# Float64 weights joined and split in pairs, and a new order for the first two halves of the program

## The chip, the core and the metric

The kernel runs on one core of one Trainium2 chip. The metric is the time of one execution on the device, in microseconds (us); the figure quoted is the median of several runs. Five engines take part: TensorE (PE in the profile, with its weight loads as PEld), VectorE (DVE), ScalarE (ACT), GpSimd (POOL) and SyncE (SP), which only issues DMAs. Each engine works through its own queue in the order in which the program was written; where one needs another's result it waits on a semaphore, and everything behind it in its queue waits too.

## The reference

The computation is a linear attention with a decaying state, followed by a layer with three up-projections, a maximum over them and a down-projection:

```
B, H, S, D = 4, 8, 768, 48            # attention: r, k, v, w (B, H, S, D), u (H, D)
for t in range(S):
    cur = u * k[t] (outer) v[t]
    y[t] = r[t] @ (state + cur)
    state = w[t][:, None] * state + k[t] (outer) v[t]
x = y.transpose(0, 2, 1, 3).reshape(3072, 384)
h = max(max(x @ w1, x @ w2), x @ w3)  # w1, w2, w3: (384, 768)
out = h @ w_out                       # w_out: (768, 384)
```

The four weight matrices arrive as float64, the rest as float32.

## The kernel before

**The parts.** Time is cut into 6 chunks of 128 steps; with 4 batches that makes 24 attention units, k = 0 to 23. Four units make 512 rows of x, one of the six "halves" of the second layer. A half has 18 up groups (6 column blocks of 128 by the three matrices; a group is 3 or 9 matmuls with 512 columns) and 8 down steps. The program begins with fillers (`warmer`, L613: matmuls on a tile of zeros whose result nobody reads). The attention of units 0 to 11, all of the weights' preparation and the first two halves of the second layer are then written out in an order given by a table of step names, `PARTS`; a loop writes the other four halves afterwards.

**Attention steps** (one letter and the unit's number). On VectorE `b`, `p`, `q`, `f`, `r`: a scan backwards (L401), a floor, an inverse, a scan forwards (L416), a product (L425); `d` and `e`: the diagonal terms (L436, and on TensorE L451, two-column matmuls); `M` copies the scores into the tile `a` (L489 on VectorE, L493 on ScalarE). On TensorE `T`: transposes (L504), `X`: scores (L482), `U`: gain of the state (L538 or L529), `R`: the state's part of the result (L517), `V` and `Y`: the two parts of scores times values (L572), with a small copy on ScalarE (`touch`, L578) between them. `E` copies the result y into x on ScalarE (L590); after units 1, 3 and 7 it also sends six small DMAs x<-x (L598) that move rows within x, three from SP's queue and three from ScalarE's in the first half, all six from SP in the second. `n` and `e` load the inputs of later units. The attention units need nothing of the weights.

**Weights.** 24 chunks of 128x384, 18 for the up groups and 6 for the down steps. For each: `w` loads the raw 64-bit words into a room of 128 x 768 words (L304); `l` converts two 16- and 32-bit parts on ScalarE (L319, L320) into a tile `cv`; `c` (function `weights`) puts the sign into one part on VectorE for this chunk (`head_w`, L333), and joins the two parts of the chunk before into a float32 value (`join_w`, L344) in a further room that two neighbours share. The first four column blocks of the first half (12 up groups and 4 down chunks) multiply these float32 values with plain x ("plain" groups, steps `gd`, `gc` on 256 columns and `ge` on 512). All others need the value split in two: `s` writes the upper part on ScalarE (L132) and, one `s` later, the remainder on VectorE (L133). `FIX` is the order of the splits: the chunks that the first half needs split come first, those of the plain groups last. x itself is split by `x`.

**Rooms.** 25 rooms of 128 x 2 x 384 words are handed out from a list; `cv` has three buffers of two parts.

A plain group is written as

```
for n, (ct, (wt, part)) in enumerate((ct, term) for ct in range(KT) for term in terms):
    nc.tensor.matmul(ps[:, cols], lhsT=wt[i][:, ct * 128:(ct + 1) * 128], rhs=x[part][:, ct, cols], ...)
```

with one term if it is plain and three (L167, x_hi and x_lo) if it is split.

Of the kernel before, what the change touches and what calls it, by code (L numbers as in the profile page):

```python
# [29 lines left out]
F32 = mybir.dt.float32  # L30
# [3 lines left out]
U16 = mybir.dt.uint16  # L34
# [41 lines left out]
PARTS = """b0 w p0 W2 d0 q0 b1 w f0 p1 e0 r0 W11 R0 q1 d1 c0 T0 f1 X0 w e1 M0 W4 V0 r1 Y0 n3 d2 X1 b2 U0 p2 q2 l E0 e2 f2 c  # L76
           l M1 T1 R1 c r2 n4 c1 S0 b3 W10 V1 Y1 E1 d3 p3 R2 w X2 M2 q3 T2 f3 w U1 S1 w c2 r3 W6 w V2 e3 l Y2 c3 b4 c w W5
           X3 l E2 T3 d4 M3 n5 W3 l R3 U2 S2 l c V3 gd1 p4 w c gd0 q4 f4 t r4 gd3 Y3 l w c t w t E3 Z4 l c e4 b5 gd4 t p5
           d5 q5 T4 n6 l c c4 w gd2 gd5 l X4 U4 t f5 m4 c S4 w w M4 t U3 gc0 r5 t gc3 t c gc1 S3 l b6 c p6 R4 V4 q6 T5 t e5
           l c5 w w l Z5 X5 Y4 U5 l f6 m5 S5 c d6 c M5 Z6 gc7 gc8 c t l t n7 w E4 gd8 c ge10 t gd7 t t b7 p7 l r6 s w ge11  # L80
           w gc4 l c s e6 t d7 l T6 q7 t w c R5 f7 n8 c6 V5 X6 U6 gd6 Y5 m6 S6 w E5 r7 s t M6 e7 c x s l gc6 c T7 R6 V6 c t
           l gc2 s c X7 t U7 w Y6 E6 ge9 l t gc5 ge13 l b8 t w ge14 d8 p8 c w l s l q8 c M7 Z7 m7 S7 ge15 t ge12 t c f8 c7
           t ge16 t r8 c R7 s T8 V7 X8 U8 s n9 s t t Y7 e8 ge17 D0 E7 b9 D2 D1 p9 n10 c8 x s Z8 d9 m8 S8 s D3 M8 s q9 s D4
           D5 D6 D7 G12 b10 s f9 s G14 r9 c9 p10 G5 t T9 t s s q10 R8 n11 V8 e9 t X9 U9 f10 Y8 s G13 E8 Z10 Z9 G16 m9 S9 t
           b11 G3 d10 G15 r10 s t c10 G17 T10 t e10 p11 R9 M9 s V9 X10 U10 t Y9 t m10 S10 d11 G0 t G2 q11 t E9 f11 G1 n12
           G4 b12 r11 T11 p12 M10 X11 R10 V10 n13 t U11 q12 t t e11 d12 Z11 t f12 s G6 m11 t t S11 s r12 G8 s Y10 t M11 t
           c11 G11 t e12 s E10 G9 G10 t T12 t b13 p13 G7 q13 d13 t R11 V11 X12 s U12 Y11 t f13 n14 H0 E11 r13 c13 H2 M12 H1
           Z13 H3 Z12 H4 c12 m12 x S12 T13 H6 H5 H7 e13"""
# [5 lines left out]
FIX = [*range(3 * FR, 3 * FT), *range(3 * FT + FR, NW), *range(3 * FR), *range(3 * FT, 3 * FT + FR)]  # L94
# [14 lines left out]
def kernel(ctx: ExitStack, tc, tin, nat, u_flat, u_pair, v_t, w_flat, out, ytr):  # L109
# [16 lines left out]
    whi, wlo, wval = {}, {}, {}  # L126
    sums = const.tile([128, LINE], F32, name="sums")
# [87 lines left out]
    left, spot = {}, NW  # L215
# [6 lines left out]
    with ExitStack() as fast:  # L222
# [11 lines left out]
        cv_p = pool("cv", 3)  # L234
# [52 lines left out]
        stage = {}  # L287

        loaded, home, held = 0, {}, []
# [5 lines left out]

        def load_w():
# [5 lines left out]
            raw = raw[:, :, :].rearrange("p a b -> p (a b)")  # L302
            raw = raw.bitcast(U16) if wide else raw[:, 0:PC]
            nc.sync.dma_start(out=raw, in_=shifted(i) if wide else w_all[i])  # L304
            stage[i] = raw

        lows = {}
        begun = 0

        def low():  # L310

            nonlocal begun
            if wide and begun < NW:
                while loaded <= begun:
                    load_w()
                body = stage[begun].bitcast(U32).rearrange("p (n t) -> p n t", t=2)[:, :, 0]
                head = stage[begun].rearrange("p (n t) -> p n t", t=4)[:, :, 2]
                cv = cv_p.tile([128, 2, PC], U32, name="cv")
                nc.scalar.activation(out=cv[:, 0, :], in_=head, func=AF.Relu, scale=8.0, bias=low_end[:, :])  # L319
                nc.scalar.activation(out=cv[:, 1, :], in_=body, func=AF.Relu, scale=2.0 ** -13 * (1.0 - 1.05 * 2.0 ** -20))  # L320
                lows[begun] = cv
                begun += 1

        def head_w(i):

            if not wide:
                wval[i] = stage.pop(i)
                home.pop(i)
                return
            if i not in lows:  # L330
                low()
            head = stage.pop(i).bitcast(U32).rearrange("p (n t) -> p n t", t=2)[:, :, 1]
            nc.vector.scalar_tensor_tensor(out=lows[i][:, 0, :], in0=head, scalar=0x8000, in1=lows[i][:, 0, :],  # L333
                                           op0=ALU.bitwise_and, op1=ALU.bitwise_or)

        def join_w(i):

            if not wide:
                return
            if i % 2 == 0:  # L340
                pairs[i // 2], pair = room()
                wval.update((i + j, pair[:, j, :]) for j in range(2))
            cv = lows.pop(i)
# [28 lines left out]
        def split_w3(i):  # L372

            w = room(F32R)[1]
            whi[i], wlo[i] = w[:, 0, :], w[:, 1, :]
            split(whi[i], wlo[i], wval[i], wrest)
# [562 lines left out]
```

## Time and profile before

| | before |
|---|---|
| median of 3 runs | 404.03 us (403.25 to 404.46) |
| the profiled execution | 403.82 us |
| its span, first to last instruction | 401.9 us |
| TensorE busy in the span | 392.3 us, 98% |
| VectorE busy | 269.8 us, 67% |
| ScalarE busy | 169.7 us, 42% |
| GpSimd busy | 84.4 us, 21% |
| granted TensorE clock, mean | 0.996 |

The profile comes from one execution. "Busy" of TensorE counts the fillers as well as the work. The span is shown in 40 slices of about 10 us as tenths, and any stretch can be asked for by its own window; a timeline lists instructions in order of time, like ones merged in one row. What an engine waited for is inferred from semaphores; "issue" is a wait that no semaphore of the profile explains.

### The profile page before, as it was taken

The page shows a single profiled execution, that of the slowest core. Times are in us where ns is not written, and L with a number is a line of the kernel's source. Part 1 is how long each engine was busy: PE and PEld are TensorE (multiplying, and loading weights), DVE is VectorE, ACT ScalarE, POOL GpSimd, SP SyncE. Part 2 cuts the span into 40 slices and gives each one's busy share as a digit, 9 for nine tenths or more (in the row PEclk, how much of TensorE's full clock was granted, in tenths as well). Part 3 has the DMA queues.
Part 4 walks back from the last instruction along what each step waited for, and adds up shares of the span by engine and source line. Part 5 has one row for each costly group of instructions (what it writes and reads, how often), then busy time and mean ns, then how long its engine had stood idle before and what let it go on. Part 6 is the DMA issues. An engine that isn't in the chain of part 4 may idle for free.

```text
span 401.9 us, 10388 instructions
## 1 busy us (share of the span) xinstructions
PE 392.3 (98%) x4361; PEld 323.7 (81%) x4361; DVE 269.8 (67%) x462; ACT 169.7 (42%) x385; POOL 84.4 (21%) x90
## 2 busy tenths in 40 slices
PE   8979999899999999999999999999999999999996
PEld 3657877587688888988889988888988888988896
DVE  5989999997758987537758568758567523243420
ACT  1458676843553243514334444334533532422110
POOL 2511221713007333043123123113123100000000
PEclk9989999999999999999999999999999999999999
DMA  8949793920425262263523594523691211400001
GB/s 215 322 144 316 229 347 120 298 67 5 146 58 193 72 194 62 76 197 137 180 62 133 169 295 134 181 76 122 185 325 60 78 41 60 140 19 2 2 21 65
DMA packets 23848, 55.76 MB, mean 139 GB/s; under 512 B 3280, under 2 KB 6672, under 8 KB 23792
## 3 DMA queue, kind: packets, MB, share of 16 engines
q1 hardware_dynamic: 20160, 45.56, 36.4%
q10 hardware_dynamic: 3632, 9.44, 7.5%
q8 instruction: 36, 0.59, 0.6%
q14 instruction: 20, 0.16, 0.1%
HBM read 49.10 MB, written 4.72 MB: 134 GB/s over the span
## 4 chain that ended last, share of the span: by engine, by line
PE 92%; DVE 3%; ACT 2%; DMA 1%; issue 1%; SPq 0%; DVEq 0%; ACTq 0%
PE psm L167 58%; PE psm L201 18%; PE y L572 3%; PE y L517 3%; PE grams L482 3%; PE psm L504 2%; PE grams L529 2%; DMA tin<-in_tin_dram 1%; PE grams L201 1%; PE y L201 1%; PE psm L451 1%; DVE tin L425 1%; DVE gf L401 1%; PE psm L613 1%; DVE kr L436 1%
## 5 line engine op out<-in xcount | busy, mean ns | idle before, releaser
L167 PE MATMUL psm<-x_hi,w 128*128 128x512 f32 x576 | 184.4, 394 | 0.0
L167 PEld LDWEIGHTS psm<-x_hi,w 128*128 128x128 f32 x576 | 108.1, 188 | 23.0
L167 PE MATMUL psm<-x_lo,w 128*128 128x512 f32 x288 | 112.3, 390 | 0.0
L459 POOL TENSOR_SCALAR_AFFINE_SELECT a<-sums 64x512 f32<-64x512 f32 x48 | 45.3, 943 | 204.5 <-DVE sums L455 148.1
L152 DVE TENSOR_TENSOR m<-psm,m 128x512 f32<-128x512 f32 x64 | 43.9, 687 | 57.2 <-PE psm L167 55.1
L201 PE MATMUL psm<-w,h_hi 128*128 128x384 f32 x264 | 70.0, 361 | 0.0
L167 PEld LDWEIGHTS psm<-x_lo,w 128*128 128x128 f32 x288 | 54.1, 188 | 10.5
L201 PEld LDWEIGHTS psm<-w,h_hi 128*128 128x128 f32 x264 | 47.7, 188 | 4.9
L132 ACT CAST h_hi<-m 128x512 fp32r<-128x512 f32 x32 | 19.7, 620 | 52.2 <-DVE m L152 52.2
L201 PE MATMUL psm<-w,h_lo 128*128 128x384 f32 x116 | 38.9, 335 | 0.0
L167 PE MATMUL psm<-x,w 128*128 128x256 f32 (+1 forms) x126 | 33.5, 416 | 1.4 <-issue 1.4
L133 DVE TENSOR_TENSOR h_lo<-m,h_hi 128x512 fp32r<-128x512 f32 x32 | 22.9, 719 | 17.5 <-ACT h_hi L132 17.5
L416 DVE TENSOR_TENSOR_SCAN gf<-tin,d_fwd 112x517 f32<-112x517 f32 x24 | 32.3, 1347 | 0.2
L401 DVE TENSOR_TENSOR_SCAN gf<-tin,d_bwd 112x517 f32<-112x517 f32 x24 | 30.2, 1259 | 3.0 <-DMA tin<-in_tin_dram 2.2
L430 ACT ACTIVATE gf<-gf 112x1034 f32<-112x1034 f32 x24 | 25.6, 1069 | 14.2 <-DVE tin L425 14.2
L425 DVE TENSOR_TENSOR tin<-tin,gf 112x1024 f32<-112x1024 f32 x24 | 30.2, 1259 | 0.1
L167 PEld LDWEIGHTS psm<-x,w 128*128 128x128 f32 x126 | 23.2, 190 | 8.6 <-issue 5.4
L572 PE MATMUL y<-a,v 64*64 64x64 f32 (+3 forms) x768 | 23.6, 230 | 3.2 <-ACT touch L578 1.8
L133 DVE TENSOR_TENSOR x_lo<-x,x_hi 128x512 fp32r<-128x512 f32 x18 | 11.4, 685 | 20.4 <-ACT x_hi L132 20.4
L150 ACT COPY m<-psm 128x512 f32<-128x512 f32 x32 | 18.6, 582 | 14.9 <-PE psm L167 14.4
L572 PEld LDWEIGHTS y<-a,v 64*64 64x64 f32 (+1 forms) x768 | 18.8, 126 | 6.4 <-ACT a L493 2.5
L439 POOL TENSOR_TENSOR kr<-kr 128x384 f32<-128x384 f32 x16 | 17.6, 1098 | 27.4 <-DMA kr<-in_nat_dram 26.4
(83 smaller groups left out, 451.7 us busy)
## 6 DMA issues: line engine op xcount, KB each, us to landing
tin<-in_tin_dram SPq DMA_DIRECT2D x23, 448.0 KB, 4.7
w<-in_w_all_dram SPq DMA_DIRECT2D x25, 384.0 KB, 8.2
w<-in_w_all_dram ACTq DMA_DIRECT2D x23, 384.0 KB, 3.4
v<-in_nat_dram SPq DMA_DIRECT2D x24, 288.0 KB, 6.3
kr<-in_nat_dram SPq DMA_DIRECT2D x16, 384.0 KB, 5.3
tin<-in_tin_dram SPq DMA_DIRECT2D x23, 229.7 KB, 5.2
out_dram<-m SPq DMA_DIRECT2D x22, 192.0 KB, 2.2
x<-x SPq DMA_DIRECT2D x30, 32.0 KB, 2.0
```

Of the source, the lines that this page charges most:

```text
L132: nc.scalar.copy(out=hi, in_=src)
L133: rest = lambda: nc.vector.tensor_tensor(out=lo, in0=src, in1=hi.bitcast(F32), op=ALU.subtract)
L150: nc.scalar.copy(out=m[:, cols], in_=ps[:, cols])
L152: nc.vector.tensor_tensor(out=m[:, cols], in0=ps[:, cols], in1=m[:, cols], op=ALU.max)
L167: nc.tensor.matmul(ps[:, cols], lhsT=wt[i][:, ct * 128:(ct + 1) * 128], rhs=x[part][:, ct, cols], start=(n == 0), stop=(n == KT * len(term ...
L201: nc.tensor.matmul(pss[tt][:, 0:DM], lhsT=ht[f][:, tok], rhs=wt[FT * 3 + f][:, :], start=(f == 0 and i == 0), stop=(f == FT - 1 and i == l ...
L401: nc.vector.tensor_tensor_scan(out=g[0:112, ::-1], data0=t[0:112, 0:WC][:, ::-1], data1=d_bwd[0:112, ::-1], initial=0.0, op0=ALU.mult, op1 ...
L416: nc.vector.tensor_tensor_scan(out=prep[k]["f"][0:112, :], data0=tbuf[k % NB][0:112, 0:WC], data1=d_fwd[0:112, :], initial=0.0, op0=ALU.mu ...
L425: nc.vector.tensor_tensor(out=both[0:112], in0=both[0:112], in1=by[0:112], op=ALU.mult)
L430: nc.scalar.activation(out=flat, in_=flat, func=AF.Square, accum_out=acc[0:112, k:k + 1])
L459: nc.gpsimd.affine_select(out=a[o:o + HC, 0:H, :], in_=cs[o:o + HC, :].unsqueeze(2).broadcast_to([HC, H, HC]), pattern=[[0, H], [1, HC]], ...
L572: nc.tensor.matmul(y[o:o + m, hh, s, part * HC:part * HC + HC if one else C], lhsT=natt[k][0][q:q + 64, at:at + m], rhs=p["a"][q:q + 64, o ...
```

## The change

A room is now twice as wide (128 x 2 x 768 words) and there are 13 of them. Two neighbouring chunks, a pair, are loaded into the two halves of one room; `l` converts both with one instruction per part, one of them in place; the sign (`h`, a step of its own now) and the join (`c`) are one instruction of 768 columns each, and the joined values overwrite the first half of the pair's own room instead of going to a new one. The split takes a pair at once (`s`), and its remainder is a step of its own (`o`), after which the pair's raw room goes back to the list. `cv` has two buffers, each of a pair. `FIX` keeps its order, in pairs.

```diff
-    free = list(range(NW + 1))
+    free = list(range(NW // 2 + 1))
...
-        return i, w_p.tile([128, 2, PC], dtype, name=f"w{i}")
+        return i, w_p.tile([128, 2, 2 * PC], dtype, name=f"w{i}")
...
-        cv_p = pool("cv", 3)
+        cv_p = pool("cv", 2)
...
-            home[i], raw = room()
+            if i % 2 == 0:
+                home[i // 2], homes[i // 2] = room()
...
+                while loaded < 2 * begun:
+                    load_w()
...
+                    lows[j] = cv = cv_p.tile([128, 2 * PC], U32, name="cv")
+                    body = raw_of(j).bitcast(U32)[:, 0::2]
+                    head = raw_of(j).bitcast(U16)[:, 2::4]
+                    nc.scalar.activation(out=cv[:, :], in_=head, func=AF.Relu, scale=8.0, bias=low_end[:, :])
+                    nc.scalar.activation(out=body, in_=body, func=AF.Relu, scale=2.0 ** -13 * (1.0 - 1.05 * 2.0 ** -20))
...
+        def head_w(j):
+
+            if wide:
+                nc.vector.scalar_tensor_tensor(out=lows[j][:, :], in0=raw_of(j).bitcast(U32)[:, 1::2], scalar=0x8000, in1=lows[j][:, :],
+                                               op0=ALU.bitwise_and, op1=ALU.bitwise_or)
...
+                nc.vector.scalar_tensor_tensor(out=homes[j][:, 0, :].bitcast(U32), in0=lows.pop(j)[:, :], scalar=16,
+                                               in1=raw_of(j).bitcast(U32)[:, 0::2],
+                                               op0=ALU.logical_shift_left, op1=ALU.bitwise_or)
...
+            both = room(F32R)[1]
+            split(both[:, 1, :], both[:, 0, :], homes[j][:, 0, :], wrest)
...
-PARTS = """b0 w p0 W2 d0 q0 b1 w f0 p1 e0 r0 W11 R0 q1 d1 c0 T0 f1 X0 w e1 M0 W4 V0 r1 Y0 n3 d2 X1 b2 U0 p2 q2 l E0 e2 f2 c
+PARTS = """W1 w b0 w p0 q0 f0 d0 W16 e0 r0 b1 d1 c0 T0 p1 w W6 e1 X0 U0 q1 W1 b2 f1 p2 M0 W1 q2 W9 R0 l r1 V0 n3 X1 c1 Y0
```

`PARTS` is a new table throughout. In it TensorE has the same matmuls as before, form by form, in another order, but for the fillers: 62 instead of 57, the 16 ahead of the table and 46 in it, all of the 46 ahead of the first plain group. VectorE and ScalarE have 36 instructions fewer each (12 pairs in place of 24 chunks, three instructions on either engine). Three places of the order follow.

**The first plain group on TensorE.** The names carry numbers: v_336 and a_475 belong to unit 3, v_249 and a_359 to unit 2. Before, the first plain groups stand behind the first part of unit 3's values:

```order
L572 MATMUL y_545<-a_475,v_336 64x64
L572 MATMUL y_545<-a_475,v_336 48x64
L167 MATMUL psm_571<-x_321,w3_355 128x256 x3
L167 MATMUL psm_580<-x_321,w3_355 128x256 x3
L167 MATMUL psm_589<-x_321,w9_560 128x256 x3
```

After, the first one stands behind unit 2's gain, ahead of unit 3's transposes and of unit 2's values:

```order
L525 MATMUL psm_481<-v_249,kn_465 64x48
L525 MATMUL psm_481<-v_249,kn_465 48x48
L168 MATMUL psm_495<-x_367,w0_172 128x256 x3
L491 MATMUL psm_499<-ident_121,tin0_107 128x112 x4
L559 MATMUL y_493<-a_359,v_249 64x128
L559 MATMUL y_493<-a_359,v_249 48x128
```

So the first plain group has moved ahead of one unit's transposes, one unit's scores and three half steps of values.

**The first weights on VectorE.** Rows 24 to 32 of its queue before: the signs of chunks 0 and 1 and the join of chunk 0.

```order
L333 SCALAR_TENSOR_TENSOR cv_318<-w0_172,cv_318 128x384
L489 COPY_PREDICATED a_255<-mask_126,grams_67 128x512
L333 SCALAR_TENSOR_TENSOR cv_341<-w1_182,cv_341 128x384
L344 SCALAR_TENSOR_TENSOR w3_355<-cv_318 128x384
L425 TENSOR_TENSOR tin2_109<-tin2_109,gf_305 112x1024
L401 SCALAR_TENSOR_TENSOR gf_362<-tin0_107,d_bwd_116 112x517
L436 TENSOR_TENSOR kr_337<-tin0_107 112x512
L410 TENSOR_SCALAR d_fwd_119<-gf_362 112x4
L489 COPY_PREDICATED a_333<-mask_126,grams_67 128x512
```

Rows 25 to 31 after:

```order
L330 SCALAR_TENSOR_TENSOR cv_300<-w0_172,cv_300 128x768
L476 COPY_PREDICATED a_246<-mask_126,grams_67 128x512
L388 SCALAR_TENSOR_TENSOR gf_392<-tin0_107,d_bwd_116 112x517
L423 TENSOR_TENSOR kr_363<-tin0_107 112x512
L397 TENSOR_SCALAR d_fwd_119<-gf_392 112x4
L336 SCALAR_TENSOR_TENSOR w0_172<-cv_300,w0_172 128x768
L400 RECIPROCAL d_fwd_119<-d_fwd_119 112x4
```

Both chunks of the first pair are now joined at the queue's row 30; before, the second chunk's join stood at row 38.

**The first split group on TensorE.** Before, the last two plain groups and the first split one (x_hi, x_lo):

```order
L167 MATMUL psm_1209<-x_321,w18_748 128x512 x3
L167 MATMUL psm_1217<-x_321,w12_607 128x256 x3
L167 MATMUL psm_1221<-x_hi_1093,w4_950 128x512
L167 MATMUL psm_1221<-x_lo_1094,w4_950 128x512
L167 MATMUL psm_1221<-x_hi_1093,w4_950 128x512 x2
```

After, it stands earlier, with four of the 256-column plain groups still to come behind it:

```order
L168 MATMUL psm_996<-x_367,w5_691 128x512 x3
L168 MATMUL psm_1000<-x_367,w5_691 128x512 x3
L168 MATMUL psm_1004<-x_hi_966,w8_978 128x512
L168 MATMUL psm_1004<-x_lo_967,w8_978 128x512
L168 MATMUL psm_1004<-x_hi_966,w8_978 128x512 x2
```

On VectorE's queue the split of x that this group needs has moved from row 121 to row 88.

## Rows read from the trace of the kernel before

**Rows 1.** The page: busy time of the engines, and PE, PEclk in 40 slices.

```profile
PE 392.3 (98%) x4361; PEld 323.7 (81%) x4361; DVE 269.8 (67%) x462; ACT 169.7 (42%) x385; POOL 84.4 (21%) x90
...
PE   8979999899999999999999999999999999999996
...
PEclk9989999999999999999999999999999999999999
```

**Rows 2.** What TensorE waited for: line, releaser; us, times, longest us.

```profile
PE y L572 <- ACT touch L578: 1.8, 3, 1.2
PE psm L167 <- issue: 1.4, 1, 1.4
PE y L572 <- ACT a L493: 1.3, 2, 1.0
```

**Rows 3.** Timeline of TensorE to the first plain group: start, duration, what.

```profile
1.07 7.02 PE L613 MATMUL psm<-warm 128*128 128x512 bf16 x18 [1.07 <-POOL warm L264]
...
8.58 2.55 PE L613 MATMUL psm<-warm 128*128 128x512 bf16 x11
...
28.20 0.56 PE L572 MATMUL y<-a,v 64*64 64x128 f32 x16
28.69 0.63 PE L451 MATMUL psm<-tin,kr 112*64 112x2 f32 x16
...
30.93 0.90 PE L482 MATMUL grams<-tin 48*64 48x128 f32 x32
31.76 0.60 PE L504 MATMUL psm<-ident,tin 112*128 112x112 f32 x4
32.20 0.81 PE L613 MATMUL psm<-warm 128*128 128x512 bf16 x3
32.94 0.67 PE L538 MATMUL psm<-v,kn 128*64 128x48 f32 x16
...
34.43 4.15 PE L167 MATMUL psm<-x,w 128*128 128x256 f32 x18
```

**Rows 4.** TensorE from 34.4 to 81.4 us, by form: count, busy, mean ns, idle before.

```profile
L167 PE MATMUL psm<-x,w 128*128 128x512 f32 x18 | 8.5, 598 | 1.4 <-issue 1.4
```

**Rows 5.** Timeline of TensorE at the end of the plain groups.

```profile
79.46 2.31 PE L167 MATMUL psm<-x,w 128*128 128x512 f32 x8 [1.43 <-issue]
81.42 0.58 PE L167 MATMUL psm<-x_hi,w 128*128 128x512 f32 x1
```

**Rows 6.** Timeline of ScalarE: unit 1's result and its DMAs.

```profile
23.61 0.59 ACT L590 COPY x<-y 112x512 f32<-112x512 f32 x1 [0.68 <-PE y L572]
24.23 2.16 ACTq L598 DMA_DIRECT2D x<-x  x3
```

**Rows 7.** The page, DMA issues: count, KB each, median us to landing.

```profile
w<-in_w_all_dram SPq DMA_DIRECT2D x25, 384.0 KB, 8.2
...
x<-x SPq DMA_DIRECT2D x30, 32.0 KB, 2.0
```

**Rows 8.** Windows: PE, PEld, DVE, ACT, POOL busy (count), PEclk, DMA share, GB/s.

```profile
0.00:20.00 20.00, 18.23 (x211) 9.81 (x211) 15.87 (x24) 6.37 (x14) 8.36 (x16) 1.00 0.90 269
...
22.00:24.00 2.00, 1.02 (x48) 1.02 (x48) 2.00 (x3) 1.32 (x5) 0.00 (x0) 1.00 0.03 8
24.00:26.00 2.00, 2.00 (x30) 1.66 (x22) 1.97 (x5) 0.20 (x1) 0.00 (x0) 0.54 0.07 16
```

**Rows 9.** Timeline of VectorE: two instructions on a chunk, x's split, one join beside GpSimd.

```profile
72.77 0.55 DVE L333 SCALAR_TENSOR_TENSOR cv<-w,cv 128x384 uint32<-128x384 uint32 x1
73.23 0.55 DVE L344 SCALAR_TENSOR_TENSOR w<-cv 128x384 uint32<-128x384 uint32 x1
73.70 1.89 DVE L133 TENSOR_TENSOR x_lo<-x,x_hi 128x512 fp32r<-128x512 f32 x3
...
79.70 1.35 DVE L344 SCALAR_TENSOR_TENSOR w<-cv 128x384 uint32<-128x384 uint32 x1
```

**Rows 10.** Timeline of SP: the DMAs within x after unit 7.

```profile
98.89 3.67 SPq L598 DMA_DIRECT2D x<-x  x6
```

More of the change, by code (lines that the diff above doesn't have):

```diff
@@ L93 @@
 PIECES = dict(a=(0, 1), b=(1, 2), c=(2, 4), d=(0, 2), e=(0, 4))
-FIX = [*range(3 * FR, 3 * FT), *range(3 * FT + FR, NW), *range(3 * FR), *range(3 * FT, 3 * FT + FR)]
+FIX = [j // 2 for j in (*range(3 * FR, 3 * FT, 2), *range(3 * FT + FR, NW, 2), *range(0, 3 * FR, 2), *range(3 * FT, 3 * FT + FR, 2))]
 CS = 8
@@ L214 @@
     ps_y = ctx.enter_context(tc.tile_pool(name="ps_y", bufs=1, space=PSUM))
-    left, spot = {}, NW
+    left, spot = {}, NW // 2
     def late(tt):
@@ L307 @@
         lows = {}
-        begun = 0
         def low():
             nonlocal begun
-            if wide and begun < NW:
-                while loaded <= begun:
+            if begun < NW // 2:
+                j, begun = begun, begun + 1
+                while loaded < 2 * begun:
                     load_w()
[L316 to L343, printed above, removed]
-            nc.vector.scalar_tensor_tensor(out=wval[i].bitcast(U32), in0=cv[:, 0, :], scalar=16, in1=cv[:, 1, :],
-                                           op0=ALU.logical_shift_left, op1=ALU.bitwise_or)
-            free.append(home.pop(i))
+                if wide:
+                    lows[j] = cv = cv_p.tile([128, 2 * PC], U32, name="cv")
[3 more added lines that the diff above has]
+                    nc.scalar.activation(out=body, in_=body, func=AF.Relu, scale=2.0 ** -13 * (1.0 - 1.05 * 2.0 ** -20))
@@ L370, in check_w, with split_w3 @@
                 (nc.scalar if i else nc.sync).dma_start(out=again[0], in_=w_all[i])
[L372 to L376, printed above, removed]
-        def let_go(i):
-            fixed_w.add(i)
-            if wide and i ^ 1 in fixed_w:
-                plain = any(j < 3 * FR or FT * 3 <= j < FT * 3 + FR for j in (i, i ^ 1))
-                (held if plain and not over else free).append(pairs[i // 2])
-        wrest, pairs, fixed_w = [], {}, set()
+        def split_w3(j):
+            both = room(F32R)[1]
+            split(both[:, 1, :], both[:, 0, :], homes[j][:, 0, :], wrest)
+            whi.update((i, one_of(i, both, 1)) for i in (2 * j, 2 * j + 1))
+            return lambda: wlo.update((i, one_of(i, both, 0)) for i in (2 * j, 2 * j + 1))
+        wrest = []
         low_end = cst.tile([128, BIT], F32, name="low_end")[:, 0:1]
@@ L640, with heads, joins, fix_low @@
         at = attn()
-        done = fixed = 0
-        def weights():
+        done = joined = fixed = 0
+        def heads():
             nonlocal done
-            if done < NW:
-                while loaded <= done:
-                    load_w()
-                head_w(done)
-            if 0 < done <= NW:
-                join_w(done - 1)
+            while begun <= done:
+                low()
+            head_w(done)
             done += 1
+        def joins():
+            nonlocal joined
+            join_w(joined)
+            joined += 1
         def fix():
             nonlocal fixed
-            rest = wrest.pop(0) if wrest else None
-            if fixed < NW:
-                split_w3(FIX[fixed])
-            if rest:
+            wrest.append(split_w3(FIX[fixed]))
+            fixed += 1
+        def fix_low():
+            for rest in wrest:
                 rest()
-                let_go(FIX[fixed - 1])
-            fixed += 1
+            wrest.clear()
+            free.append(home.pop(FIX[fixed - 1]))
         units = 3 * UPH
-        xs, now, over = {}, None, False
+        xs, now = {}, None
         def judge():
@@ L722, in group @@
         def group(step):
-            nonlocal over
             if step[0] in "DH":
                 next(now["down"])
-                if step == "D7":
-                    over = True
-                    free.extend(held)
                 return
@@ L740 @@
         warmer(WARM)
-        acts = dict(w=load_w, l=low, c=weights, s=fix, x=split_x, t=lambda: now["catch_up"](1))
+        acts = dict(w=load_w, l=low, h=heads, c=joins, s=fix, o=fix_low, x=split_x, t=lambda: now["catch_up"](1))
         for step in PARTS.split():
```

50 lines of the change are left out of this document (28 added, 22 removed).

## The prediction

> **What bounds the kernel now.** I began with busy time and the slices: TensorE is busy in 98% of the span, at full clock in nearly all of it [rows 1]. That says little by itself, because "busy" counts the fillers. The second view was what TensorE waited for: under 5 us in all, of which only one wait, 1.4 us, stands at L167, the second layer's groups [rows 2]. The third was its timeline. Up to 34.4 us the queue holds attention steps of units 0 to 3 and fillers; then the first plain group starts [rows 3]. From there to 81.4 us, where the first split group starts, the groups' only idle time is that 1.4 us [rows 4, 5]; the slices behind it are full. So the program has two parts: a start of 34.4 us, in which TensorE waits for the scans on VectorE and fills the time, and 367 us in which it works without a pause. The matmuls are the same, form by form, in both kernels. **The time is therefore set by how much of TensorE's time is lost**, and nearly all of the loss lies ahead of the first plain group. What the change saves on VectorE and ScalarE counts only where it brings that group forward or closes a gap behind it.
>
> **The change part by part.** *When the first plain group can start.* It needs three things: its place in TensorE's queue, the weights of pair 0, and x of units 0 and 1.
>
> Queue: 33 fillers come first. The 18 before end at about 8.0 (the clock rises on the way); the next 11 took 2.55 us, 0.23 each [rows 3], so 15 more end at 11.4. Then, up to unit 0's first values: two L451 of 0.6, a transpose of 0.45 (31.76 to 32.20), 6 fillers (1.3), scores of 0.83 (30.93 to 31.76), the gain of 0.67 and 11 fillers (2.4) [rows 3]: 11.4 + 1.2 + 0.45 + 1.3 + 0.83 + 0.67 + 2.4 = 18.2. Then half the values (0.49, from 28.20 to 28.69), scores (0.83), values (0.49), transpose (0.45), L451 (0.6), 6 fillers (1.3), gain (0.67): 23.0. Unit 1's values are two halves with the touch between them, 0.49 + 0.3 (the shorter of the three waits for it, (1.8 - 1.2) / 2 [rows 2]) + 0.49: 24.3. Behind them scores, L451, transpose, 6 fillers, gain: 3.9, so 28.2.
>
> x: unit 1's copy follows its values, 24.3 to 24.9 (0.59). Three DMAs on each of two queues are issued in 2.16 us, the last at about +1.5, and land 2.0 us after that [rows 6, 7]: 28.4.
>
> Weights: VectorE's 30th instruction joins pair 0. Before, 24 had been started by 20.0 us, and the next eight came in about four [rows 8]; with the two wider ones it ends at about 24.5. That is hidden.
>
> So the first plain group starts at 28.4 instead of 34.4, **6.0 us earlier**. But it has overtaken work that was done ahead of it before: one unit's transposes (0.45), one unit's scores (0.83) and three half steps of values (3 x 0.49 = 1.5), together **2.75 us**. Net: 6.0 - 2.75 = **3.3 us less lost**.
>
> *The fillers.* Five more, about 1.1 us on TensorE, all inside the 28.4 us, so they are in the sum already. They also bear on the clock. Before, TensorE was busy for 1.02 of the 2 us from 22 to 24, and the clock then fell to 1.2 GHz, shown as 0.54 of full between 24 and 26 [rows 8]. After, the idle time between 20 and 24 comes to about half a microsecond by the walk above, so I expect no fall. The Trainium skill, "TensorE: Matmul & The Clock Gate", Part 1, calls half rate the default state, which activity releases. The row agrees with that; were the new order's small matmuls not to count as enough activity, the clock would fall as before, and that case is a rival below.
>
> *The gap of 1.4 us at 78 to 79.5.* It lies inside a group, between matmuls whose tiles two others had just read, and the profile ties it to no semaphore [rows 5]. If it was a late weight or buffer, it goes: the queue there is another one. If it was something of the queue itself, it may return. Bounds 0 and 1.4; nothing in the rows is nearer to either, so I take the middle, **0.7 us**.
>
> *The wider instructions.* On VectorE two neighbours start 0.46 us apart for 384 columns [rows 9]. x's split takes 0.60 for 512 ((1.89 - 0.09) / 3, the overhang of 0.55 over 0.46 taken off) [rows 9]. That is 1.1 ns a column and 0.04 us fixed, so 768 columns take 0.88 and a pair saves 0.04 per step: 36 x 0.04 = 1.4 us over the whole program. Hidden behind TensorE, it is worth nothing directly. What it does is keep VectorE ahead: x's split stands at row 121 before (start 73.7 us) and at row 88 after. Ahead of it lie 37 weight instructions before (37 x 0.46 = 17.0 us) and 14 after (14 x 0.88 = 12.3), and ten fewer others, some 5.5 us; so it starts at about 73.7 - 4.7 - 5.5 = 63.5, and the first split weights are whole at about 67. TensorE, without a pause from 28.4 on, comes to the first split group at about 69 (the 47 us from 34.4 to 81.4 less four 256-column groups of 1.4 and the gap). Cover: 2 us. ScalarE saves likewise and was busy 42% [rows 1]; its three DMA issues hold it for 2.2 us at the same place in the sequence as before.
>
> *Loads and rooms.* A pair's conversion waits for its second chunk, and a load takes 8.2 us to land [rows 7]. For pair 2 (needed at about 39.5) the second load is issued near 27.5 and lands near 35.7; conversion, sign and join then take about 3.5, so 39.2: just in time. Loss 0 to 1.5; I take 0 because VectorE and ScalarE are ahead of TensorE at the later pairs. The loads wait for rooms only at pairs 10 and 11, wanted by the down steps near 90: cover about 10 us.
>
> *From half 0 to half 1.* x of unit 7 is copied (0.6), moved by six DMAs from SP (3.67 us for all [rows 10], 2.0 to land) and split (about 1.2 for a third); the first third is ready 5.7 us after unit 7's values, the last 7.0. TensorE's order leaves it the rest of two output tiles, a gain and a transpose there, about 6.3 us, and it needs the last third only 1.3 us later. Nothing lost, or up to 1.
>
> **The sum:** 403.82 (the profiled execution) - 3.3 - 0.7 = 399.8. That execution lies 0.2 below the median of 404.03, so the forecast is **399.9 us**.
>
> **The rivals.**
> *The clock falls early.* If the stretch around 24 to 28 runs at 1.2 GHz, the scores, L451, transpose, 6 fillers and gain there take up to twice their time; what outlasts x's landing at 28.4 is put on top, 1.3 to 2 us: 401.2 to 402. For it: small matmuls with few columns lie in this stretch as before. Against: the idle time is gone. Chance 0.12.
> *The gain is handed back.* TensorE starts early, then stands for pair 2 or 3, or for x of units 2 and 3, because the loads bound these: 8.2 us a load against a need that now comes 5 to 6 us sooner. One to three such waits of 1 us: 401 to 403; all of it, 403.9. For it: the just-in-time sum above. Chance 0.2, a third of it within 0.3% of no change.
> *The wide instructions cost far more than two narrow ones; slower.* They step over two words per element across a double room, and one writes over what it reads. No row shows such a form; the nearest bad row is a join of 1.35 us beside a busy GpSimd [rows 9], which per pair would be 2.7 instead of 0.88. Fourteen of them precede the first split group: 14 x 1.8 = 25 us against a cover of 2, so 403.8 - 4 + 23 = 423. It decides from (2 + 4) / 14 = 0.43 us more each, 1.3 us per wide instruction; below that it only eats the gain. Against: the sign already reads every second word at the same 0.46 us. Chance 0.08.
> *More than forecast.* The 1.4 us gap goes whole and the touches' waits [rows 2] shrink too: 398.3. Chance 0.1.
>
> **How the numbers follow.** Forecast (399.2 to 400.8) 0.5, clock 0.12, handed back 0.2, more 0.1, slower 0.08. Faster by over 0.3% (1.2 us, about what a measurement can tell from no change): 0.5 + 0.12 + 0.13 + 0.1 = 0.85, of which I keep 0.82 since a table of steps this long may hide a wait that I did not walk; within 0.3%: 0.1; slower: 0.08. The range must reach the clock's case and most of the second: 398.0 to 403.0, leaving out the slow case and the end of the second, some 0.16 above, and a little below.
>
> **What the profile after would show.** The first L167 or L168 matmul at about 28.4 us and no idle time of it before 81 but perhaps one "issue"; PEclk without a fall in the third slice; wide instructions of about 0.97 us (0.88 from start to start) on VectorE; x's split at about 63.5 us and the first split group near 69. The forecast is wrong if the first plain group comes after 31, if TensorE stands at weights or x between 35 and 50, or if wide instructions take over 1.3 us.

## The result and the profile after

Beside each other, the changed kernel took 399.18 us (398.21 to 400.11, 4 runs) and the kernel before 404.25 us (403.25 to 406.04, 4 runs): a ratio of 0.9853, 95% interval 0.9817 to 0.989. Measured twice more on other chips it came to 0.9906 (0.9875 to 0.9937) and 0.9861 (0.9835 to 0.9887); weighted by their intervals, 0.987. That is 4 to 6 us faster; 399.9 had been predicted.

The profiled execution of the changed kernel took 400.11 us, with a span of 398.3 us. The page's lines on TensorE look as before [rows 1]:

```profile
PE 388.6 (98%) x4366; PEld 322.5 (81%) x4366; DVE 267.2 (67%) x426; ACT 164.8 (41%) x349; POOL 90.9 (23%) x90
...
PE   8989899999999999999999999999999999999994
...
PEclk9999999999999999999999999999999999999999
```

TensorE's timeline (start, duration, what, in brackets the idle time before and its releaser) answers [rows 3] and [rows 5]:

```profile
1.07 8.82 PE L600 MATMUL psm<-warm 128*128 128x512 bf16 x33 [1.07 <-POOL warm L265]
...
26.62 0.67 PE L525 MATMUL psm<-v,kn 128*64 128x48 f32 x16 [0.56 <-ACT kn L493]
27.22 1.56 PE L168 MATMUL psm<-x,w 128*128 128x256 f32 x6
...
67.06 0.79 PE L168 MATMUL psm<-x_hi,w 128*128 128x512 f32 x1
```

The first plain group starts at 27.22 us (before 34.43), the first split group at 67.06 (before 81.42). The granted clock, by windows (us, PE busy, PEld, DVE, ACT, POOL, PEclk, DMA share, GB/s), does not fall where it fell before [rows 8]:

```profile
22.00:24.00 2.00, 1.66 (x70) 1.49 (x62) 2.00 (x4) 0.97 (x3) 0.65 (x1) 1.00 0.90 252
24.00:26.00 2.00, 2.00 (x19) 1.08 (x16) 2.00 (x4) 0.12 (x2) 0.00 (x0) 1.00 0.25 76
```

What TensorE waited for (line, releaser: us in total, times, longest), against [rows 2]:

```profile
PE y L559 <- ACT touch L565: 0.9, 3, 0.3
PE psm L525 <- ACT kn L493: 0.6, 1, 0.6
PE psm L168 <- DVE w L336: 0.5, 1, 0.5
PE psm L438 <- issue: 0.4, 1, 0.4
PE psm L438 <- DVE h_hi L153: 0.4, 1, 0.4
```

The 1.4 us of "issue" at L167 is gone from the plain groups. New are the wait of 0.6 us at L525, just ahead of the first plain group, and the last three, 1.3 us together, that all lie between 41 and 43.8 us.

**Where the time came from.** Both kernels have the same matmuls but for fillers. So for each trace I took the start of a matmul and subtracted the usual intervals (the mean of the middle 80% over all traces of this study) of the matmuls before it, fillers counted as nothing. What is left is TensorE's time lost so far, in us:

| at | before | after | after, 2nd profile | after, 3rd profile |
|---|---|---|---|---|
| 27 us | 21.0 | 19.8 | 20.5 | 20.2 |
| 35 us | 25.4 | 20.8 | 21.3 | 21.0 |
| 45 us | 26.1 | 23.5 | 24.0 | 23.6 |
| 60 us | 27.0 | 24.2 | 24.5 | 24.1 |
| 80 us | 30.8 | 24.5 | 24.8 | 24.4 |
| 120 us | 36.4 | 30.6 | 30.6 | 30.4 |
| the last matmul | 44.2 | 38.7 | 38.8 | 38.2 |

At one time the kernels stand at different places in their work, so single steps between 45 and 120 us are to be read with care. Still: 4.4 us are won by 35 us, 2 are given back by 45, the rest comes by 80, and at the end 5.4 to 6.0 us are left. Of the 3.8 us that the kernel before loses between 60 and 80, the gap of [rows 5] is 1.6. No other interval there is more than 0.2 us over its usual length: what remains is spread over the changes from one small form to the next, which the table counts as lost too. The spans of the kernel before and of the first profile after differ by only 3.6 us, because the time behind the last matmul was 3.6 us before and 5.4 after. That part is the same code and scatters between executions of one kernel (last section).

### The profile page after: what moved, and what is told of

Read it like the earlier page. It is cut to its first block, busy times and chain, and to the rows that moved or that the text cites. A ratio compares the mean times of both kernels' runs of the same rounds, so it can differ in the third digit from the quotient of the medians.

```text
span 398.3 us, 10319 instructions
## 1 busy us (share of the span) xinstructions
PE 388.6 (98%) x4366; PEld 322.5 (81%) x4366; DVE 267.2 (67%) x426; ACT 164.8 (41%) x349; POOL 90.9 (23%) x90
## 4 chain that ended last, share of the span: by engine, by line
PE 85%; DMA 6%; DVE 4%; issue 2%; ACT 1%; SPq 1%; POOL 1%; ACTq 0%; DVEq 0%; POOLq 0%
PE psm L168 54%; PE psm L202 17%; DMA tin<-in_tin_dram 4%; PE y L504 3%; PE y L559 3%; PE psm L600 2%; PE grams L469 2%; DMA kr<-in_nat_dram 1%; PE grams L516 1%; PE psm L491 1%; PE grams L202 1%; PE y L202 1%; DMA x<-x 1%; DVE cv L330 1%; PE psm L438 0%
## 5 line engine op out<-in xcount | busy, mean ns | idle before, releaser
L446 POOL TENSOR_SCALAR_AFFINE_SELECT a<-sums 64x512 f32<-64x512 f32 x48 | 47.5, 989 | 191.2 <-DVE sums L442 124.4
L133 ACT CAST h_hi<-m 128x512 fp32r<-128x512 f32 x32 | 19.8, 620 | 49.0 <-DVE m L153 48.9
L403 DVE TENSOR_TENSOR_SCAN gf<-tin,d_fwd 112x517 f32<-112x517 f32 x24 | 30.1, 1255 | 0.2
L426 POOL TENSOR_TENSOR kr<-kr 128x384 f32<-128x384 f32 x16 | 20.4, 1274 | 28.7 <-DMA kr<-in_nat_dram 26.4
L565 ACT COPY touch<-y 112x4 f32<-112x4 f32 x24 | 3.9, 163 | 50.8 <-PE y L559 50.8
```

The lines of the kernel that those rows point to most:

```text
L133: nc.scalar.copy(out=hi, in_=src)
L403: nc.vector.tensor_tensor_scan(out=prep[k]["f"][0:112, :], data0=tbuf[k % NB][0:112, 0:WC], data1=d_fwd[0:112, :], initial=0.0, op0=ALU.mu ...
L426: nc.gpsimd.tensor_tensor(out=n[:, 0, :], in0=n[:, 0, :], in1=n[:, 1, :], op=ALU.mult)
L446: nc.gpsimd.affine_select(out=a[o:o + HC, 0:H, :], in_=cs[o:o + HC, :].unsqueeze(2).broadcast_to([HC, H, HC]), pattern=[[0, H], [1, HC]], ...
```

## The experiments

Ratios are to the kernel before on the same chip, with 95% intervals. The changed kernel's own, for comparison, is 0.987.

| kernel | ratio |
|---|---|
| narrow instructions, new order | 0.9948 (0.9925 to 0.9971) |
| wide instructions, old order | 1.005 (1.0012 to 1.0088) |
| before, two groups for fillers | 1.001 (0.9982 to 1.0039) |
| the same, code shifted | 0.9971 (0.9944 to 0.9999) |
| before, 8 fillers fewer | 1.0056 (1.0028 to 1.0083) |
| after, without 46 fillers | 0.9951 (0.9926 to 0.9976) |
| after, no sign on VectorE | 0.9883 (0.9838 to 0.9927) |
| after, unit 5's loads earlier | 0.9882 (0.9851 to 0.9913) |
| after, unit 6's loads later | 0.9889 (0.9861 to 0.9916) |

**1. Narrow instructions in the new order.** Each 768-column instruction on the weights is cut in two, on both engines; rooms and table stay. One of the cut places, shortened:

```diff
-                nc.vector.scalar_tensor_tensor(out=lows[j][:, :], in0=raw_of(j).bitcast(U32)[:, 1::2], ...)
+                for o in (slice(0, PC), slice(PC, 2 * PC)):
+                    nc.vector.scalar_tensor_tensor(out=lows[j][:, o], in0=raw_of(j).bitcast(U32)[:, 1::2][:, o], ...)
```

> The new order with every wide instruction cut into two of 384 columns again: 36 instructions more on VectorE and on ScalarE, all else as in the changed kernel. Theory (the time follows from what TensorE loses ahead of and just behind its first plain group; the wide instructions only give VectorE cover): VectorE has 1.4 us more work over the program, of which the first plain group sees 0.1, so it starts at 27.2 to 27.6 us and the time is 399 to 400 us. Rival (the gain comes from the cheaper wide instructions): most of it goes, 402.5 to 404.5 us.

Measured: 402.76 us beside 405.13, ratio 0.9948. The theory's 399 to 400 was too low; the time lies in the rival's range. The order alone brings about 2 us and the wide form 2 to 4 more (0.9948 against the changed kernel's 0.985 to 0.991), though VectorE was thought to be hidden. Its timeline, in the changed kernel and then in this one, at the split of x and the first split weights:

```profile
61.46 1.90 DVE L134 TENSOR_TENSOR x_lo<-x,x_hi 128x512 fp32r<-128x512 f32 x3
65.59 0.97 DVE L134 TENSOR_TENSOR w<-w,w 128x768 fp32r<-128x768 f32 x1
```

```profile
64.06 2.79 DVE L134 TENSOR_TENSOR x_lo<-x,x_hi 128x512 fp32r<-128x512 f32 x3
69.24 1.01 DVE L134 TENSOR_TENSOR w<-w,w 128x384 fp32r<-128x384 f32 x2
```

With wide instructions the first split weights are whole at 66.6, half a microsecond ahead of TensorE's 67.06. With narrow ones they come 3.7 us later, and TensorE's first split group starts at 69.59. That costs nothing yet: the first matmul to read what VectorE writes here is the group's third, and TensorE has no idle time at this group in either trace. Compared matmul by matmul with the second profile of the changed kernel, TensorE is 2.2 us late before the group and within it alike, and 4.0 us late at 109 us. What it loses behind the group lies mostly at two transposes that wait for a product on VectorE (0.75 us here and 0.2 us at 107.94), in the narrow kernel alone:

```profile
88.86 0.60 PE L496 MATMUL psm<-ident,tin 112*128 112x112 f32 x4 [0.75 <-DVE tin L417]
```

That product on VectorE, in the narrow kernel and then in the changed one, where the same transposes start at 84.98, 0.65 us behind it (0.4 and 0.8 us in the other two profiles):

```profile
87.59 1.22 DVE L417 TENSOR_TENSOR tin<-tin,gf 112x1024 f32<-112x1024 f32 x1
```

```profile
83.11 1.22 DVE L412 TENSOR_TENSOR tin<-tin,gf 112x1024 f32<-112x1024 f32 x1
```

VectorE has no idle time over 0.25 us from 45 to 88 us in any profile of the changed kernel, so it has next to nothing to spare there. In the narrow kernel it also waits twice for ScalarE's conversions, which were cut as well (0.55 us at 50.33, 0.42 at 51.31). How the 2 to 4 us divide between the two engines' narrow instructions stays open.

In this profile the clock also fell to half from 44.8 to 48.2 us, behind a stand of 1.6 us. TensorE loses 1.7 us in that stretch. How much of it is left of the 3.6 by which the last matmul is later than in the second profile stays open, since VectorE too was held up behind ScalarE's copies of these slow groups. The fall is luck of the execution: the mean clocks over the runs are alike (0.9973 here, 0.9972 in the changed kernel's ten).

**2. Wide instructions in the old order.** Double rooms and wide instructions, with the old table; a pair's step stands where its second chunk's stood.

```diff
-... p2 q2 l E0 e2 f2 c l M1 T1 R1 c r2 n4 ...
+... p2 q2 E0 e2 f2 l M1 T1 R1 h c r2 n4 ...
```

> The wide instructions and double rooms in the order of the kernel before: each pair's conversion, sign, join and split stand where the first kernel had those of one of its two chunks, all other steps, fillers included, where they were. Theory: the first plain group stays behind the first half of unit 3's values and starts at 33.5 to 35 us; 403 to 405 us. Rival (the wide instructions carry the gain): 399 to 401 us.

Measured: 407.85 us beside 405.13, ratio 1.005, slower. The theory expected no loss; the first plain group starts at 35.54 us. In the old order a pair begins only with its second chunk, and VectorE waits longer for ScalarE's conversion than before (0.6 us at most):

```profile
45.30 0.96 DVE L318 SCALAR_TENSOR_TENSOR cv<-w,cv 128x768 uint32<-128x768 uint32 x1 [1.59 <-ACT cv L312]
```

TensorE then stands for VectorE twice, at 84.91 and at 97.22 us, where the kernel before has no wait:

```profile
PE psm L156 <- DVE h_hi L141: 1.6, 1, 1.6
PE psm L479 <- DVE tin L400: 1.2, 1, 1.2
```

These 2.7 us are more than the 2.0 that the ratio gives, but the profile is of the slowest of seven executions (410.4 us), and that the late conversion led to both waits is not shown. So order and width are no sum: -0.5% and +0.5% each alone, -1.3% together.

**3. The kernel before, two groups for fillers.**

```diff
-... c3 b4 c w W5 X3 l E2 T3 d4 M3 n5 W3 l R3 U2 S2 l c V3 gd1 p4 w c gd0 ...
+... c3 b4 c w gd0 X3 l E2 T3 d4 M3 n5 gd1 l R3 U2 S2 l c V3 p4 w c ...
```

> The kernel before with two plain groups, gd0 and gd1, put where 5 and 3 fillers stood at 29.7 and 32.2 us, and the fillers taken out; nothing else moved. Theory: two groups of 1.38 us are done in time that was lost; the fillers took 2.0 us, so unit 3's first values come 0.7 us later and the net is 2.0 us: 401.8 to 402.6 us. Rival (TensorE's early time is worth nothing because VectorE limits the stretch up to 81 us anyway): 403.7 to 404.5 us.

Measured: 405.5 us beside 405.13, ratio 1.001. A miss: the first plain group started at 29.37 us and the lost time at 35 us was 1.8 us less than before (23.6 against 25.4), but at 60 us 2.4 us more (29.4 against 27.0). TensorE's timeline there:

```profile
51.77 0.55 PE L529 MATMUL grams<-v,kn 64*64 64x48 f32 x21
53.55 0.66 PE L529 MATMUL grams<-v,kn 64*48 64x48 f32 x11 [1.23 <-issue]
54.14 4.12 PE L167 MATMUL psm<-x,w 128*128 128x256 f32 x12
```

It stood in the middle of a row of like matmuls, for nothing that a semaphore explains, and then ran 12 plain matmuls in 4.12 us instead of some 2.8, at half clock (53.3 to 56.7 us). Besides, it waited for VectorE at 35.30 (0.6 us), 38.86 (1.0) and 94.41 (1.0).

**4. What "issue" is.** TensorE's program comes to it in packets of 16 KB, on a queue of their own on the DMA engines (queue, kind: packets, MB, share):

```profile
q8 instruction: 36, 0.59, 0.7%
```

36 packets for 4,366 matmuls and as many weight loads make some 120 matmuls a packet; the places of the stands give about 127. They lie behind the 1,103rd matmul before, the 724th in experiment 3, the 596th in the changed kernel and in experiment 1: 596 + 127 = 723, and 3 x 127 more make 1,104. Counted so, a packet starts when TensorE has entered the packet before (the count is good to some 15 matmuls): within 1 us of that where the DMA engines are idle, and up to 9 us later where they are full. Two such stretches of experiment 3, from TensorE's entry to the start of the next packet (windows, columns as above, the DMA share next to last):

```profile
53.55:62.89 9.34, 9.34 (x40) 6.92 (x41) 7.10 (x15) 5.05 (x12) 1.39 (x1) 0.83 1.02 287
69.13:69.90 0.77, 0.77 (x59) 0.71 (x52) 0.77 (x4) 0.77 (x3) 0.77 (x1) 1.00 0.00 0
```

Seven of the eight "issue" stands of 1 us or more in all traces lie where one packet ends and the next has just landed; TensorE goes on 1.2 to 1.6 us after the landing (77.93 to 79.46 before, 52.24 to 53.55 in experiment 3). The eighth, 1.6 us at 11.91 in experiment 3, lies ahead of the first packet (17.04) and stays open. The next run tests it.

```diff
-WARM = 16
+WARM = 8
```

> The kernel before with 8 fillers fewer at its very start (8 instead of 16 ahead of the table); nothing else differs. Theory: the gap of 1.4 us at 78 to 79.5 us is TensorE waiting for its own code. A 16 KB packet on the instruction queue started at 76.92 us, one matmul ahead of the gap, and the gap ended 1.5 us after it had landed. Code then comes in pieces of some 127 matmuls with their weight loads, and with 8 matmuls fewer in front each piece ends 8 matmuls later in the work. Those 8 take 0.43 us each at that place, 3.4 us, so the code is there in time and the gap goes: some 1.5 us less than the kernel before, unless another piece now ends in a row of small matmuls (the 722nd matmul is the nearest case, with 0.3 us to spare). Rival: the gap belongs to the group in which it lies (a weight, a buffer of PSUM, a reader of it); then it stays between the same two tiles with the same 1.4 us, and the time is that of the kernel before within 0.5 us.

Measured: 407.06 us beside 404.15, ratio 1.0056. The gap left its place, and a like one opened at the place named as the nearest case, behind the 723rd matmul:

```profile
52.50 0.50 PE L529 MATMUL grams<-v,kn 64*64 64x48 f32 x20
54.49 0.43 PE L529 MATMUL grams<-v,kn 64*48 64x48 f32 x12 [1.50 <-issue]
...
77.86 4.14 PE L167 MATMUL psm<-x,w 128*128 128x512 f32 x12
```

Twelve plain matmuls, among them those that stood before, now run through. So the place belongs to the count of instructions and not to the group, and the rival (a weight, a buffer) is out. That the kernel got 2.3 us slower was not foreseen: the clock takes some 0.8 of it (mean 0.9933 against 0.9954; TensorE now waits 1.9 us at the start, and the clock fell from 9.2 to 12.7 us). A new wait for VectorE of 1.0 us, at a transpose at 93.86, is there as in experiment 3 and not in the kernel before; what brought it, and the remainder, stay open.

Then experiment 3 again, with 30 two-column matmuls at the start, which only shift the packets:

```diff
+        shift(30)   # 30 matmuls psum[:, 0:2] <- warm, warm[:, 0:2]
```

> The kernel before with two plain groups (gd0, gd1) in place of the fillers W5 and W3, as in an earlier run that brought no gain, and now 30 two-column matmuls on the tile of zeros behind the 16 first fillers, at the very start. They cost some 0.04 us each where TensorE only fills, and they make every piece of TensorE's code (some 127 matmuls) end 30 matmuls earlier in the work. In the earlier run the piece that ended at the 722nd matmul was run through in 2.8 us, and TensorE stood 1.4 us for the next one; then the clock fell from 53.3 to 56.7 us. By that run's timeline the pieces now take 10.1, 9.5, 7.8, 6.9, 17, 3.9 and 5.4 us, the short ones (near 72 and 78 us) at a time with few loads. Theory: the gain missing there went to that stand and to the fall of the clock behind it; with both gone the time is 1.5 to 3 us less than in that run, a ratio of 0.993 to 0.997 to the kernel before. Rival: the stands are VectorE's (its waits of 0.8 and 1.1 us at 34.5 and 37.7 us); then the ratio is 1.001 again.

Measured: 404.37 us beside 405.32, ratio 0.9971, 0.4% under experiment 3 and at the upper end of what was expected:

```profile
50.98 0.68 PE L529 MATMUL grams<-v,kn 64*64 64x48 f32 x32
51.59 5.87 PE L167 MATMUL psm<-x,w 128*128 128x256 f32 x22
...
75.43 0.25 PE L529 MATMUL grams<-v,kn 64*64 64x48 f32 x1 [1.03 <-issue]
```

The 32 matmuls now run through in 0.68 us; another stand, of 1.0 us, came up behind the 1,104th, and the clock did not fall. So some 1.6 of the 2.4 us that were missing in experiment 3 had gone with the stand at a packet's end and what followed it; the intervals of the two ratios overlap, so the size is rough. The waits for VectorE at 34.50 (0.6 us) and 38.06 (1.0) stayed; the one at 94 is gone.

**5. The stand near 42 us in the changed kernel.** The changed kernel was measured and profiled again:

> The changed kernel once more, beside the kernel before, as a measure for the other runs of this call. The first measurement gave a ratio of 0.9853 to the kernel before. If that holds on this chip, the ratio lies between 0.982 and 0.989, some 6 us under the kernel before; if part of it was the luck of a few runs, between 0.989 and 0.995.

Measured: 400.62 us beside 404.15, ratio 0.9906, in the second of the two ranges: part of the first ratio was the luck of a few runs. In this profile the stand is one wait for code (the first had 0.4 us of it and two waits on VectorE, whose scan had waited for unit 5's input):

```profile
41.40 0.63 PE L438 MATMUL psm<-tin,kr 112*64 112x2 f32 x14
43.53 0.22 PE L438 MATMUL psm<-tin,kr 112*64 112x2 f32 x2 [1.51 <-issue]
```

TensorE had entered the packet before at 35.6 us; the next one ran from 41.0 to 42.1. Two runs moved loads on SP's queue. First unit 5's inputs ahead of the weights:

```diff
-... b4 e3 T2 w l W6 f3 ... U3 e4 r4 n5 h gd3 ...
+... b4 e3 T2 n5 w l W6 f3 ... U3 e4 r4 h gd3 ...
```

> The changed kernel with the two loads of unit 5's scan input issued right after unit 2's transposes, ahead of three loads of weights and one of values on SP's queue, instead of behind them. The profile after shows VectorE waiting 1.55 us for this input at 38.8 us, and TensorE standing for some 1.8 us between 40.6 and 43.8. Theory (that stand is the load's): VectorE's wait goes and TensorE's with it, 1.3 to 2 us less than the changed kernel: 397.2 to 398.2 us. Rival (the stand is that of pair 3's weights, which now land 2 us later): 399 to 400 us, and the wait moves to the weights' conversion on ScalarE.

Measured: 400.5 us beside 405.13, ratio 0.9882, no gain over the changed kernel. The wait only moved, as the rival had it. ScalarE now waits 3.18 us for pair 2's weights, and TensorE for what stands behind that on ScalarE's queue:

```profile
36.87 0.98 ACT L324 ACTIVATE cv<-w,low_end 128x768 uint32<-128x768 uint16 x1 [3.18 <-DMA w<-in_w_all_dram]
```

```profile
39.10 0.62 PE L516 MATMUL grams<-v,kn 64*64 64x48 f32 x30 [1.97 <-ACT kn L493]
```

Then unit 6's inputs and one load of weights behind the DMAs within x:

```diff
-... c X4 n6 U4 b5 d5 t Y3 gd2 w E3 c4 w gd4 ...
+... c X4 U4 b5 d5 t Y3 gd2 E3 n6 w c4 w gd4 ...
```

> The changed kernel with two steps of SP's queue moved: the two loads of unit 6's inputs and one load of weights stand behind the x<-x DMAs after unit 3 instead of ahead of them (issued at about 41 us instead of 32.7 to 34.4). Nothing else differs. Theory: the stand of 1.5 us at 41.8 to 43.5 us in the second run of the changed kernel is TensorE's wait for a piece of code whose packet, asked for at about 35.6 us, ran only from 41.0 to 42.1 because it queued behind these loads; with 3 of the loads gone (some 1.06 MB, about 3 us of the DMA engines) it runs at about 38 and the stand is gone. Unit 6's scan comes 1 to 1.5 us later on VectorE, which has that to spare. 1 to 1.7 us less than the changed kernel, a ratio of about 0.987. Rival: the packet's start does not depend on the loads; then the stand stays, and the later loads cost up to 1 us: ratio 0.991 to 0.994.

Measured: 400.55 us beside 405.32, ratio 0.9889; the changed kernel beside them 399.55 us, 0.9861:

> The changed kernel a third time, beside the two others of this call. The two measurements so far gave ratios of 0.9853 and 0.9906; between 0.985 and 0.992 is expected, and its profile shows whether the stand near 42 us has 0.4 us, as in the first, or 1.5 us, as in the second.

This third profile of the changed kernel has 0.54 us of waiting for code at 43.09 and 0.45 at 36.09. In the kernel with the loads moved the packet ran at 37.8 to 38.8 us, as foreseen, and L438 went through:

```profile
42.55 0.63 PE L438 MATMUL psm<-tin,kr 112*64 112x2 f32 x16
...
47.40 2.86 PE L168 MATMUL psm<-x,w 128*128 128x256 f32 x12 [0.71 <-DVE h_hi L153]
```

But unit 6's scan then waited for its input, more than the 1 to 1.5 us allowed for, and the groups waited behind it on VectorE's queue:

```profile
45.79 1.24 DVE L388 TENSOR_TENSOR_SCAN gf<-tin,d_bwd 112x517 f32<-112x517 f32 x1 [2.61 <-DMA tin<-in_tin_dram]
```

So between 30 and 50 us something that the DMA engines bring is late in each of these five traces: code, a unit's input or a pair of weights. Which it is depends on the order, and these two exchanges won nothing. That is not the engines' bandwidth alone. In this run they are nearly idle from 38 to 42 us (next to last column), and unit 6's loads, behind the DMAs within x on SP's queue, are issued only after that:

```profile
38.00:40.00 2.00, 2.00 (x32) 1.78 (x24) 1.92 (x3) 2.00 (x4) 0.36 (x1) 1.00 0.04 12
40.00:42.00 2.00, 2.00 (x11) 1.77 (x10) 2.00 (x7) 0.16 (x1) 0.00 (x0) 1.00 0.10 25
...
42.06 1.40 SPq L262 DMA_DIRECT2D tin<-in_tin_dram  x2
```

Whether loads that are issued in that gap, from another queue, would win the 2 us was not tried.

**6. The fillers.** The changed kernel without its 46 fillers in the table.

```diff
-PARTS = """W1 w b0 w p0 q0 f0 d0 W16 e0 r0 b1 d1 c0 T0 p1 w W6 e1 ...
+PARTS = """w b0 w p0 q0 f0 d0 e0 r0 b1 d1 c0 T0 p1 w e1 ...
```

> The changed kernel without the 46 fillers of its table (the 16 ahead of the table stay). Theory: the first plain group's time is set by x, which follows from VectorE's scans, so it still starts at about 27 us; the fillers only fill, but without them TensorE idles for some 10 us in all ahead of it, its clock falls there as it did in the kernel before at 24 to 27.6 us, and the small matmuls and the first groups run at half rate: 1 to 3 us slower than the changed kernel. Rival: the clock falls no oftener than with them; then the time is the same within 1 us, or up to 1 us less since the small matmuls stand behind no filler. Besides, if the stand of 0.4 us at 42.4 us is TensorE waiting for its own code, that comes in pieces, the piece's end lies 46 matmuls later in the work here and this stand is gone from its place.

Measured: 402.24 us beside 404.15, ratio 0.9951, and 1.6 us more than the changed kernel measured beside it (3 by the weighted ratio). The clock stayed at 1.2 GHz from about 10 to 34 us (a window, columns as above; then the first plain group in TensorE's timeline, 2.93 us for six matmuls instead of 1.56):

```profile
20.00:30.00 10.00, 7.81 (x125) 6.86 (x124) 10.00 (x14) 5.33 (x14) 4.50 (x4) 0.50 0.60 188
```

```profile
29.47 2.93 PE L156 MATMUL psm<-x,w 128*128 128x256 f32 x6
```

With the fillers in, the clock did not fall in this stretch in any profile of the changed kernel. The Trainium skill, "TensorE: Matmul & The Clock Gate", Part 1, calls half rate the default, released by activity; the rows agree. That the price is no higher shows how much of this stretch TensorE spends waiting in any case: the group comes 1.6 to 2.2 us later, not twice as late. The stand for code near 42 us is gone from its place, as expected with 46 matmuls fewer in front.

**7. VectorE relieved.** The 12 sign instructions are left out (the weights then have no sign).

```diff
-            if wide:
+            if wide and j < 0:
                 nc.vector.scalar_tensor_tensor(out=lows[j][:, :], ...)
```

> The changed kernel without its 12 sign instructions on VectorE (the weights lose their sign; nothing else is left out). It takes 12 x 0.87 = 10.4 us from VectorE's queue, four times the 1.4 us and more that the wide instructions were reckoned to save, most of it ahead of 95 us. Theory: TensorE is the bound and VectorE's work is hidden but for the stand near 40 to 44 us, where the loads come late anyway; 0 to 1.5 us less than the changed kernel. Rival: VectorE's queue sets the pace of the first two halves; then 4 us less or more.

Measured: 399.96 us beside 404.15, ratio 0.9883: the theory. Some 10 us less on VectorE (257.6 us busy against 267.3) bring nothing clear of the noise, while 4.6 us more (271.9 in experiment 1, where ScalarE has 4 us more too) go with a loss of 2 to 4. With the product of experiment 1 ready 0.4 to 0.8 us ahead of its use, the wide form takes VectorE just below the point at which it binds.

## Why the prediction was right, and where its steps were not

*What bounds the kernel.* Right: TensorE's lost time ahead of the first plain group was what there was to win. By 35 us, 4.4 us are won.

*The first plain group.* 28.4 us was forecast, 27.2 to 27.9 came. The walk took the first fillers from [rows 3], where the clock rose at 7.1 us; in the three profiles after it rose between 3.8 and 5.5. Two experiments with the same start whose clock rose at 6.8 had the group at 28.5. So the walk was right for its clock. The net gain of 3.3 us was 1.1 less than the table's 4.4.

*The gap of 1.4 us.* Counted half, not knowing its cause. It is code, and it went whole: that matmul started 2.0 us after the one before, 1.6 over the usual 0.43. The choice of a middle value was no working; what would have told was the packet of code, in the trace of before one matmul ahead of the gap.

*Loads and rooms: "loss 0 to 1.5; I take 0".* This step failed. Between 35 and 45 us the changed kernel loses 2.7 us and the kernel before 0.7, so 2 us go back. TensorE's idle time there, 1.3, 1.5 and 1.0 us in the three profiles, lies within the bounds; the choice of 0 was wrong, and so was the cause. In these profiles TensorE did not stand for pair 2, as reckoned, but for what else the DMA engines bring in that stretch: its own code in all three profiles, and in the first pair 3's join, 0.5 us at 43.79, held up on VectorE behind a scan that waited 1.55 us for unit 5's input. That last one is a stand at weights between 35 and 50, which the prediction had named as a sign of being wrong. The rival "the gain is handed back" came true in part. The other rival, "more than forecast", did so too: the gap went whole, and the waits for the touches and for `a` [rows 2] shrank from 3.1 us to 1.1.

*The wide instructions.* The price was right, 0.88 us from one start to the next, 0.96 in duration (VectorE's timeline after):

```profile
34.66 0.96 DVE L330 SCALAR_TENSOR_TENSOR cv<-w,cv 128x768 uint32<-128x768 uint32 x1 [0.54 <-ACT cv L324]
35.54 0.80 DVE L544 TENSOR_TENSOR sstar<-scur,dec 112x192 f32<-112x192 f32 x1
```

That rules out the slower rival. "Worth nothing directly" was wrong in its effect. The cover at the first split group was 0.5 us (weights whole at 66.6, group at 67.06) and not the 2 reckoned, but no run shows TensorE standing there. Where VectorE runs out of cover is at the transposes near 85 us, a place that the prediction did not walk: 0.4 to 0.8 us to spare with the wide form, 0.75 us of waiting without it (experiment 1). x's split began at 61.5 us (63.5 forecast), the first split group at 67.06 (69, from a sum that took in neither the 2.75 us of overtaken work nor the small steps that moved behind this group).

*The clock.* No fall, as expected [rows 8]; experiment 6 shows the price of a fall over a longer stretch (10 to 34 us), 1.6 to 3 us against the rival's 1.3 to 2.

*Half 0 to half 1.* Taken as 0; from 80 us on the changed kernel gives back 0.6 us by the table.

In sum 3.3 + 0.7 was forecast; 4.4 to 35 us, 2.0 back, 1.6 for the gap and some 1.4 that no single wait accounts for make 5.4 on TensorE. The nearness of 399.9 to 399.2 owes something to two errors that offset each other.

## What to carry to other kernels

Where an engine seems full, count the time it loses ahead of its useful work, subtract what a group overtakes, and then ask what the DMA engines must bring in the time that is now shorter. Treat TensorE's code as one of those loads: ahead of the stands above, TensorE ran through a packet in 3 to 7 us, and the next was late where the DMA engines were full. A change of a few in the count of instructions can move such a stand, or open one, without any change in the work (8 fillers in experiment 4). And look at an engine that never idles, even where nobody waits for it yet: VectorE's cover here was 0.4 to 0.8 us.

## What the runs showed of the hardware

- *Code.* The Trainium skill, "Runtime: NRT & Kernel Launch", section "Instruction fetch mechanics", says that code comes in 16 KiB blocks of 256 instructions and that crossing into a new one is mostly hidden. The packets' size and count agree; the crossing was not hidden where the DMA engines were full: 1.0 to 1.9 us in seven traces.
- *The end.* The last 192 KB to DRAM landed 1.9 or 4.1 us after their issue, in two executions of the same changed kernel (third profile, then second; columns: KB, us to landing). A difference of 2 us between two profiled spans can be that alone.

```profile
out_dram<-w SPq DMA_DIRECT2D x1, 192.0 KB, 1.9
```

```profile
out_dram<-w SPq DMA_DIRECT2D x1, 192.0 KB, 4.1
```

- *The clock's rise.* In the first fillers it rose between 3.8 and 7.1 us after the start, whatever the kernel; 33 fillers took 8.8 us with an early rise, and with the late one of [rows 3] the first 18 alone took 7.0.
